# A new order table for every step of a one-core attention and gated-MLP kernel, with its range flag made and loaded ahead of the end

## The chip, the cores and the metric

The kernel runs on one core of one Trainium2 chip. The metric is device microseconds (us) of one execution, as the median of several; the kernel before took 780.11 us in the median of three runs (779.42 to 783.94). Engines are called as in the profile: PE (TensorE, matrix products), PEld (its weight loads), DVE (VectorE), ACT (ScalarE), POOL (GpSimd), SP (SyncE, which issues most DMAs).

## The reference

Eight sequences of 448 tokens, 12 heads of 64. Attention with RMS-normed queries and keys, then a gated MLP with a convolution of three taps along the sequence.

```python
q_n, k_n = rmsnorm(q, g_q), rmsnorm(k, g_k)            # over head_dim = 64
scores = 1 / sqrt(64) * q_n @ k_n.T
attn = exp(scores - max); attn /= attn.sum + 1e-9
x = (attn @ v) heads side by side                       # 8 x 448 x 768
h = relu(x @ w_in)                                      # 768 -> 1024
conv = conv_w[0]*h[t-1] + conv_w[1]*h[t] + conv_w[2]*h[t+1]
out = (h * sigmoid(conv)) @ w_out                       # 1024 -> 768
```

## The kernel before, in words

The unit of attention is a pair of heads of one sequence; there are 48 pairs, six to a sequence, numbered n = 0 to 47. For each pair the kernel loads q, k and v, squares and sums them (`square`, `square_sum`), makes 1/rms in nine small steps (`rsqrt`), scales (`apply_rms`), turns q and k so that the head dimension lies across partitions (`qk_transpose` on PE with `qk_hi`, `qk_lo`; from pair 10 on q by a DMA, `q_hi`, `q_lo`, `q_turn`), forms the scores (`scores`, L862), takes the exponent with a fixed shift (`soft_exp`, L887, on ACT), turns the probabilities, and multiplies by v (`pv`, L1031). Pairs 0 to 9 keep float32 and turn the probabilities on PE (`p_transpose` L939, `p_evac`). Pairs 10 to 47 split every number into two float16 parts (`p_hi`, `p_lo`) and turn them with one DMA per 128 queries (`p_turn`, L931, issued by SP). The row sums are inverted, stored to DRAM and loaded back spread over the partitions (`sum_store`, `sum_load`, `sum_spread`), and `x_scale` applies them.

The MLP of sequence b takes the six finished pairs: `in_part` (L1120) forms x @ w_in for one of eight blocks of 128 features in three float16 products, `in_relu`, `in_conv`, `in_tanh` and `in_gate` make the gated value, `in_hi`, `in_lo` split it, `out_part` (L1189) forms the output for 128 tokens and 384 columns, `out_evac` scales it and `out_store` (L1203) sends it out. Since 448 is three and a half blocks of 128 tokens, the last 64 tokens of an even sequence wait in `carry` and share a block with the first 64 of the next.

PE uses its array in three ways. Products with 128 rows and 128 columns of weights fill it (`in_part`, most of `out_part`, the transposes). `scores` contracts over 64, so two products run at once, one in each half of the rows (64\*128 in the profile, and 64\*64 where a group is half as wide). `pv`, and the block that two sequences share, have 64 columns of weights, so two products run at once, one in each half of the columns (128\*64).

Nothing is scheduled at run time. `plan_qk`, `plan_v`, `plan_attention`, `plan_moe` and `plan_weight` list all 4614 steps, and the string `ORDER` then says, with four characters a step, which step comes next, on which engine it runs and which of the eight PSUM banks it takes. Each engine runs its own steps in that order, and an engine (SP and the ACT queue too, as issuers of DMAs) that must wait holds all that stands behind it. The weights come in at the start as 512 KB pieces (`load`, L438), in 64-bit words whose parts `convert` puts together on DVE.

The attention uses a fixed shift in the exponent; the largest and smallest row sums say afterwards whether that was in range. `sum_check`, `range_turn` (one PE transpose of `top`, L378) and `range_top` (one DVE reduction, L381) make one number of it; `values_load` (L1395) reads it into a register of every engine, and a branch (L1396) skips a general version of the whole kernel, whose code lies between that branch and the end.

```python
    flag = nc.values_load(top[0:1, 2:3].bitcast(I32), min_val=0, max_val=0x7FFFFFFF)
    with tc.If(flag > 0x3F800000):
        general = True
```

Of the kernel before, what the change touches and what calls it, by code (L numbers as in the profile page):

```python
# [9 lines left out]
I32 = mybir.dt.int32  # L10
# [10 lines left out]
    "$2&!$3&!$v&!$w&!$4$!$?$!$x$!%&$!!6&!!!#!$5#!$6#!%^&!$7#!!7&!!0&!!8&!$@#!$P&!$8%!$9%!$y#!$:#!%(#!"  # L21
    "%_&!$A%!$B#!$;#!$z#!%)#!%8&!%r&!$C#!%*#!$<#!$D#!$=#!$E#!%+#!$>#!$F#!${#!%,#!$G#!$|#!!9&!$H#!$J#!"
    "$K!#$I#!!?#!$M#!&:&!!:#!$N!$!1#!$}%!$L$!$O$!$R!B!@#!$~#!$U$!%-#!!;#!!A#!!<#!!>&!!C&!$Q#!%!#!%9#!"
    "&;&!&D&!%.%!%#%!%$#!!D#!!B$!$S!V%%#!$T!l$V!#%s#!%a$!%/%!%0#!!E#!%1#!!I#!!F#!%5#!!J#!%2%!$X$!!=$!"
    "$[$!$_$!%b#!$Y!$!N#!!K#!$]!%&~&!!H&!!M&!(P&!&k&!!O#!$W$!%6!&$Z$!$^$!%7$!!S#!!T#!!P#!!R&!!U#!!W&!"
    "$c$!$f$!%3!(%4$!$a!)$b$!&<$!&=#!%:!.%;!B%<!l$d!($g!)$i$!$l%!$m#!!L$!%>$!%c%!$n#!%d#!!X#!%e#!%f#!"
    "!Y#!%g#!!Z#!!Q$!%h#!%i%!$e$!$h#!%j#!!^#!%k#!%o%!%l%!&E#!(!#!$j!#(Q#!!_#!(R#!%=!:!a#!$o&!!]&!!c&!"
    "!V$!#(&!%A$!!d#!&A#!#)&!(F&!$k$!$p&!$q&!!h#!!e#!!i#!&l&!(G&!)2&!%?!%%B!#%D$!%E!&%@$!%G$!%C$!%H!)"
# [1400 lines left out]
```

## Time and profile before

| | |
|---|---|
| median of three runs | 780.11 us |
| profiled execution, its own time | 784.36 us |
| its span, first to last instruction | 782.6 us |
| PE busy | 749.9 us, 96% |
| DVE busy | 657.2 us, 84% |
| ACT busy | 625.7 us, 80% |
| POOL busy | 345.2 us, 44% |
| granted TensorE clock, mean | 0.996 of full speed |
| DMA, mean | 167 GB/s |

The profiled execution is 4.25 us longer than the median of the runs, and 1.76 us of it lie outside the span. A busy PE is not a PE at its peak: the ends of products are modelled, and a product that starts late inside a run of them shows only in the distance of the starts. Times in the rows are microseconds from the span's start; "xN" merges N like instructions that follow each other; what stands in brackets is idle time before the row and what ended it.

### The profile page before, as it was taken

The page shows a single profiled execution, that of the slowest core. Times are in us where ns is not written, and L with a number is a line of the kernel's source. Part 1 is how long each engine was busy: PE and PEld are TensorE (multiplying, and loading weights), DVE is VectorE, ACT ScalarE, POOL GpSimd, SP SyncE. Part 2 cuts the span into 40 slices and gives each one's busy share as a digit, 9 for nine tenths or more (in the row PEclk, how much of TensorE's full clock was granted, in tenths as well). Part 3 has the DMA queues.
Part 4 walks back from the last instruction along what each step waited for, and adds up shares of the span by engine and source line. Part 5 has one row for each costly group of instructions (what it writes and reads, how often), then busy time and mean ns, then how long its engine had stood idle before and what let it go on. Part 6 is the DMA issues. An engine that isn't in the chain of part 4 may idle for free.

```text
span 782.6 us, 16529 instructions
## 1 busy us (share of the span) xinstructions
PE 749.9 (96%) x5279; PEld 400.0 (51%) x5279; DVE 657.2 (84%) x1592; ACT 625.7 (80%) x1482; POOL 345.2 (44%) x538
## 2 busy tenths in 40 slices
PE   3899999999999989999999999999999999999996
PEld 1455555455545545555545554455445554555553
DVE  6998999999889989898899878997899878974731
ACT  3999899989899868898899778987998778970511
POOL 0154436654366126552465524663465435731200
PEclk9999999999999999999999999999999999999999
DMA  9986664598999999999999999999999988783002
GB/s 239 268 207 185 164 133 96 110 183 185 184 191 185 204 182 180 168 176 206 188 188 187 195 193 184 199 186 180 189 167 180 194 188 155 143 148 83 11 1 85
DMA packets 353428, 130.93 MB, mean 167 GB/s; under 512 B 295708, under 2 KB 349748, under 8 KB 353332
## 3 DMA queue, kind: packets, MB, share of 16 engines
q1 hardware_dynamic: 342928, 120.64, 81.0%
q10 hardware_dynamic: 10404, 9.15, 4.6%
q8 instruction: 43, 0.70, 0.4%
q14 instruction: 53, 0.43, 0.2%
HBM read 48.20 MB, written 11.80 MB: 77 GB/s over the span
## 4 chain that ended last, share of the span: by engine, by line
PE 64%; ACT 13%; DMA 9%; DVE 6%; issue 4%; SPq 1%; POOL 1%; ACTq 0%; DVEq 0%; POOLq 0%
PE bank L1189 23%; PE bank L1120 18%; PE bank L1031 10%; PE bank L862 9%; DMA PT<-PT 3%; DMA PT<-ph 3%; PE bank L939 3%; PE bank L681 2%; ACT PT L267 1%; DMA qkf<-in_q_dram 1%; ACT sq L600 1%; ACT ph L267 1%; DVE ph L279 1%; ACT wi L457 1%; DMA gqk<-in_g_k_dram 1%
## 5 line engine op out<-in xcount | busy, mean ns | idle before, releaser
L1120 PE MATMUL bank<-x,wi 128*128 128x448 f16 x1152 | 229.6, 354 | 2.1 <-DVE kT L731 0.7
L1189 PE MATMUL bank<-wo,gring 128*128 128x384 f16 (+1 forms) x1056 | 196.2, 327 | 0.0
L1120 PEld LDWEIGHTS <-wi 128*128 128x128 f16 x1152 | 111.1, 98 | 109.8 <-issue 14.9
L1189 PEld LDWEIGHTS <-gring 128*128 128x128 f16 (+1 forms) x1056 | 101.4, 99 | 68.3 <-issue 14.2
L862 PE MATMUL bank<-kT,qT 64*128 64x448 f16 (+3 forms) x1072 | 126.4, 388 | 6.1 <-ACT e_(19_2_3546 L887 1.9
L1031 PE MATMUL bank<-PT,vp 128*64 128x448 f16 x836 | 86.7, 354 | 1.0 <-DMA PT<-ph 0.5
L279 POOL TENSOR_TENSOR sq<-qkf,st 112x512 f32<-112x512 f32 (+1 forms) x44 | 46.1, 1060 | 53.5 <-DVE st L637 13.5
L1031 PEld LDWEIGHTS <-vp 128*64 128x64 f16 x836 | 46.2, 110 | 38.9 <-issue 11.7
L862 PEld LDWEIGHTS <-qT 64*128 64x128 f16 (+1 forms) x912 | 33.7, 97 | 56.9 <-issue 34.4
L600 ACT ACTIVATE sq<-qkf 128x1024 f32<-128x1024 f32 (+2 forms) x49 | 49.5, 1022 | 6.6 <-DMA qkf<-in_k_dram 4.5
L681 PE MATMUL bank<-ident,sq 128*128 128x128 f32 (+1 forms) x232 | 35.3, 277 | 13.8 <-DVE st L637 11.1
L609 DVE TENSOR_REDUCE st<-sq 128x16 f32<-128x1024 f32 x38 | 45.3, 1211 | 2.6 <-ACT sq L600 2.6
L1189 PE MATMUL bank<-wo,wi 128*128 128x384 f16 (+1 forms) x192 | 46.9, 326 | 0.0
L279 POOL TENSOR_TENSOR qkf<-sq,qkf 112x512 f16<-112x512 f32 x26 | 30.1, 1162 | 24.6 <-ACT c_(1_0_2529 L271 6.3
L681 PEld LDWEIGHTS bank<-ident,sq 128*128 128x128 f32 (+1 forms) x232 | 26.8, 143 | 24.4 <-issue 16.0
L1189 PE MATMUL bank<-wo,carry 128*64 128x384 f16 x192 | 35.5, 329 | 0.0
L279 DVE TENSOR_TENSOR sq<-qkf,st 112x512 f32<-112x512 f32 (+1 forms) x52 | 34.7, 695 | 0.3
L1031 PE MATMUL bank<-PT,v 112*64 112x448 f32 x160 | 32.3, 545 | 0.0
L774 DVE TENSOR_REDUCE vacc<-v 128x1 f32<-128x512 f32 (+1 forms) x48 | 31.6, 675 | 0.3
L1189 PE MATMUL bank<-wo 128*128 128x384 f16 (+1 forms) x96 | 31.3, 326 | 0.0
L1042 DVE TENSOR_TENSOR x<-bank,rB 128x448 f32<-128x448 f32 x38 | 23.6, 622 | 9.1 <-PE bank L1031 7.7
L279 POOL TENSOR_TENSOR x<-x,x 128x448 f16<-128x448 f32 x22 | 22.8, 1037 | 17.4 <-DVE x L267 4.8
(1911 smaller groups left out, 1714.2 us busy)
## 6 DMA issues: line engine op xcount, KB each, us to landing
qkf<-in_q_dram SPq DMA_DIRECT2D x18, 448.0 KB
wo<-in_moe_w_in_dram SPq DMA_DIRECT2D x12, 512.0 KB
gring<-in_moe_w_out_dram SPq DMA_DIRECT2D x16, 384.0 KB
v<-in_v_dram SPq DMA_DIRECT2D x17, 256.0 KB
qkf<-in_k_dram SPq DMA_DIRECT2D x16, 256.0 KB
qkf<-in_k_dram SPq DMA_DIRECT2D x17, 192.0 KB
PT<-ph SPq DMA_TRANSPOSE x178
qkf<-in_k_dram SPq DMA_DIRECT2D x10, 224.0 KB
```

The costliest lines, as they stand in the source:

```text
L267: (nc.scalar.copy if e == "ACT" else elementwise(e).tensor_copy)(dst, src)
L279: elementwise(e).tensor_tensor(dst, a, b, op=op)
L600: nc.scalar.activation(sq, x, AF.Square)
L609: nc.vector.tensor_reduce(st, sq, axis=AX.X, op=ALU.add)
L681: nc.tensor.transpose(ps[:, t * w : (t + 1) * w], x[:, t], ident[:w, :w])
L774: nc.vector.tensor_reduce(keyed(n, old("vacc", b))[:, i : i + 1], keyed(n, old("v", n)).rearrange("p h t d -> p (h t d)"), axis=AX.X, op=A ...
L862: nc.tensor.matmul(ps[u][o, :S], lhs, rhs, start=(i == 0), stop=(whole(m) or i == 2),)
L939: nc.tensor.transpose(ps[:w, kt * P : (kt + 1) * P], e[:, kt * w : (kt + 1) * w], ident)
L1031: nc.tensor.matmul(ps[HALF[h], :S], lhs, pt[:, k, h * S : (h + 1) * S], start=(i == 0 and j == 0), stop=(i == pvs(n)[-1] and j == NB - 1),)
L1042: nc.vector.tensor_tensor(x, ps, r, op=ALU.mult)
L1120: nc.tensor.matmul(ps[:, :S], wi[:, wl, c, fc * P : (fc + 1) * P], old("x", b * NP + c)[:, xl], start=(i == 0), stop=(i == 3 * NP - 1),)
L1189: nc.tensor.matmul(ps[p0 : p0 + m, :NO2], g, wo[:, wl, fc, half * NO2 : (half + 1) * NO2], start=(i == 0), stop=(i == 3 * NFC - 1),)
```

## The change

`ORDER` is written anew: all 4614 steps and the arithmetic stay, nearly every one stands elsewhere (by 15 places in the mean), 381 steps run on another engine, and banks are given anew. By kind the engines' shares hardly move: `p_hi` has 216 steps on ACT instead of 218 and 37 on POOL instead of 29, `apply_rms` 55 on DVE instead of 52, `out_store` 34 on SP instead of 30, `v_load` 15 on ACT's queue instead of 10. The check of the range stands ahead of the last products of the last sequence, and the register is loaded 30 steps before the end, without the test of its bounds. From the new code on, line numbers are higher by one, and from the moved load on by up to six.

```diff
 ORDER = (
-    "$2&!$3&!$v&!$w&!$4$!$?$!$x$!%&$!!6&!!!#!$5#!$6#!%^&!$7#!!7&!!0&!!8&!$@#!$P&!$8%!$9%!$y#!$:#!%(#!"
...
 WHOLE = 10
 QTURN = 10
+LATE = 30
 SPREAD = 10
...
     with tc.manual_schedule():
-        for step, fn in order:
+        for i, (step, fn) in enumerate(order):
+            if i == len(order) - LATE:
+                flag = nc.values_load(
+                    top[0:1, 2:3].bitcast(I32),
+                    skip_runtime_bounds_check_because="a float that is not negative",
+                )
             taken[:] = placed[step]
...
-    flag = nc.values_load(top[0:1, 2:3].bitcast(I32), min_val=0, max_val=0x7FFFFFFF)
     with tc.If(flag > 0x3F800000):
```

The first place is SP at the start of the program. Before, the first DMAs stand so; `gqk` are the two gain vectors, which every k of the first pair must be multiplied by, and `wo32` is the buffer in which the pieces of w_in arrive.

```order
L562 DMA qkf0_76<-in_k_dram 112x2x256
L578 DMA qkf0_76<-in_q_dram 112x4x128
L562 DMA qkf1_77<-in_k_dram 112x2x256
L576 DMA qkf1_77<-in_q_dram 112x2x128 x2
L438 DMA wo32_84<-in_moe_w_in_dram 128x1024
L562 DMA qkf2_78<-in_k_dram 112x2x256
L438 DMA wo32_84<-in_moe_w_in_dram 128x1024
L1236 DMA gqk_67<-in_g_q_dram 64x1 x2
L1236 DMA gqk_67<-in_g_k_dram 64x1 x2
```

Now the same stretch reads as follows.

```order
L563 DMA qkf0_76<-in_k_dram 112x2x256
L563 DMA qkf1_77<-in_k_dram 112x2x256
L579 DMA qkf0_76<-in_q_dram 112x4x128
L577 DMA qkf1_77<-in_q_dram 112x2x128 x2
L439 DMA wo32_84<-in_moe_w_in_dram 128x1024 x2
L563 DMA v_79<-in_v_dram 112x2x256
L439 DMA wo32_84<-in_moe_w_in_dram 128x1024
L1237 DMA gqk_67<-in_g_q_dram 64x1 x2
L1237 DMA gqk_67<-in_g_k_dram 64x1 x2
```

Three pieces of w_in stand ahead of the gains instead of two, and a load of v in place of a load of k of the same size.

The second place is PE in the first pairs, from the last scores of pair 0 (`kT_177`) through those of pair 1 (`kT_275`); L939 are transposes of probabilities. Before:

```order
L862 MATMUL bank<-kT_177,qT_179 64x448 x2
L862 MATMUL bank<-kT_275,qT_259 64x448 x2
L862 MATMUL bank<-kT_275,qT_259 128x448 x4
L939 MATMUL bank<-ident,e_(0_4_267 112x128 x4
L939 MATMUL bank<-ident,e_(0_5_269 112x128 x4
L939 MATMUL bank<-ident,e_(0_6_301 112x128 x4
L862 MATMUL bank<-kT_275,qT_259 128x448 x2
```

Now, with the same tiles under other numbers:

```order
L863 MATMUL bank<-kT_174,qT_185 64x448 x2
L863 MATMUL bank<-kT_236,qT_228 64x448 x2
L863 MATMUL bank<-kT_236,qT_228 128x448 x2
L940 MATMUL bank<-ident,e_(0_4_264 112x128 x4
L940 MATMUL bank<-ident,e_(0_5_289 112x128 x4
L940 MATMUL bank<-ident,e_(0_6_292 112x128 x4
L863 MATMUL bank<-kT_236,qT_228 128x448 x2
L940 MATMUL bank<-ident,e_(1_0_298 112x128 x4
L940 MATMUL bank<-ident,e_(1_1_314 112x128 x4
L940 MATMUL bank<-ident,e_(1_2_319 112x128 x4
L682 MATMUL bank<-ident,sq_207 128x112 x8
L863 MATMUL bank<-kT_236,qT_228 128x448 x2
```

The scores of pair 1 come in three visits between full-array transposes instead of two. Counted over the whole program, two products that follow each other on PE have different shapes of the array 273 times before and 317 times now.

The third place is the end of SP's program, with the last output stores, the register load and the branch. Before:

```order
L1203 DMA out_0_dram<-c_('o'_7_0_0_9965 128x384
L1203 DMA out_0_dram<-c_('o'_7_3_1_9969 128x384
L1203 DMA out_0_dram<-c_('o'_7_1_1_9972 128x384
L1203 DMA out_0_dram<-c_('o'_7_3_0_9977 128x384
L1395 TENSOR_LOAD top_92
L1395 ISA x2
L1396 COMPARE_AND_BRANCH
```

Now:

```order
L1204 DMA out_0_dram<-c_('o'_7_2_1_9861 128x384
L1385 TENSOR_LOAD top_92
L1204 DMA out_0_dram<-c_('o'_7_3_1_9875 128x384
L1204 DMA out_0_dram<-c_('o'_7_1_0_9898 128x384
L1204 DMA out_0_dram<-c_('o'_7_0_1_9909 128x384
L1204 DMA out_0_dram<-c_('o'_7_1_1_9942 128x384
L1204 DMA out_0_dram<-c_('o'_7_3_0_9940 128x384
L1204 DMA out_0_dram<-c_('o'_7_0_0_9986 128x384
L1401 COMPARE_AND_BRANCH
```

Six of the last stores now stand behind the load; the two instructions of the bounds test are gone, and the branch follows the last store. On PE the load now stands between two products of the last 100, and the transpose of `top` further ahead; nothing follows the last product but the branch.

## Rows read from the trace of the kernel before

**Rows 1.** The page: span, and busy time by engine with its share.
```profile
span 782.6 us, 16529 instructions
PE 749.9 (96%) x5279; PEld 400.0 (51%) x5279; DVE 657.2 (84%) x1592; ACT 625.7 (80%) x1482; POOL 345.2 (44%) x538
```

**Rows 2.** Stretches: us, busy by engine (instructions), granted clock, DMA share, GB/s.
```profile
15.00:40.00 25.00, 21.66 (x121) 12.12 (x123) 24.12 (x57) 23.22 (x63) 4.37 (x9) 1.00 0.93 267
40.00:200.00 160.00, 158.53 (x1054) 87.51 (x1051) 148.56 (x358) 150.27 (x360) 82.89 (x113) 1.00 0.70 157
200.00:400.00 200.00, 195.62 (x1415) 101.50 (x1414) 176.46 (x427) 174.18 (x412) 91.27 (x151) 0.99 1.06 188
400.00:600.00 200.00, 196.27 (x1454) 102.69 (x1454) 179.56 (x423) 175.85 (x417) 105.64 (x172) 1.00 1.05 185
600.00:775.00 175.00, 175.00 (x1235) 94.47 (x1232) 119.60 (x289) 96.64 (x225) 59.64 (x84) 1.00 0.59 118
```

**Rows 3.** PE's waits, 40 to 775 us: us in total, times, longest.
```profile
PE bank L862 <- ACT e_(19_2_3546 L887: 1.9, 1, 1.9
...
PE bank L1031 <- DMA PT<-ph: 0.5, 1, 0.5
PE bank L862 <- DMA qT<-qkf: 0.4, 1, 0.4
```

**Rows 4.** ACT's waits, 40 to 700 us, the two longest.
```profile
ACT ph L267 <- DMA PT<-ph: 10.1, 7, 5.0
ACT e_(19_2_3546 L887 <- DMA rd<-rT: 5.5, 1, 5.5
```

**Rows 5.** PE in order of time, two stretches: start, us, engine, line, tiles, shape, count.
```profile
501.26 2.27 PE L1031 MATMUL bank<-PT,vp 128*64 128x448 f16 x22
503.46 5.85 PE L1120 MATMUL bank<-x,wi 128*128 128x448 f16 x30
509.15 0.60 PE L681 MATMUL bank<-ident,sq 128*128 128x128 f32 x4
...
692.70 1.88 PE L862 MATMUL bank<-kT,qT 64*128 64x448 f16 x18
694.50 2.27 PE L1031 MATMUL bank<-PT,vp 128*64 128x448 f16 x22
696.71 11.88 PE L1189 MATMUL bank<-wo,gring 128*128 128x384 f16 x72
```

**Rows 6.** The start: the chain's wait for the gains, the order of time, DMA rate, a piece's size.
```profile
6.75 6.16 DMA gqk<-in_g_k_dram
...
13.34 0.15 DVE L1239 TENSOR_TENSOR G<-gqk 128x1 f32<-128x1 f32 x1
14.88 4.16 PE L862 MATMUL bank<-kT,qT 64*128 64x448 f32 x12 [0.67 <-ACT qT L267]
...
4.00:13.00 9.00, 0.98 (x4) 0.67 (x4) 6.20 (x29) 2.49 (x5) 0.61 (x3) 1.00 1.00 271
...
wo<-in_moe_w_in_dram SPq DMA_DIRECT2D x12, 512.0 KB
```

**Rows 7.** The end: last product and store; load and branch by line, ns min/median/max, first start.
```profile
775.27 0.33 PE L1189 MATMUL bank<-wo 128*128 128x384 f16 x1
...
776.29 0.33 SPq L1203 DMA_DIRECT2D out_dram<-c_('o'_7_3_0_9977  x1
...
L1395 PEldq TENSOR_LOAD <-top x1: 487/487/487, 776.1 to 776.1; - x1
L1395 SPq TENSOR_LOAD <-top x1: 531/531/531, 776.7 to 776.7; - x1
...
L1396 PEldq COMPARE_BRANCH  x1: 4422/4422/4422, 776.7 to 776.7; - x1
...
L1396 SPq COMPARE_BRANCH  x1: 57/57/57, 777.6 to 777.6; - x1
```

**Rows 8.** SP's own waits: issues of q's turn held by scores of an earlier pair.
```profile
SPq L723 <- PE bank L862: 9.1, 5, 6.5
```

More of the change, by code (lines that the diff above doesn't have):

```diff
@@ new lines @@
+    "$Q#!$}%!$~#!!=$!$X$!%!#!%a$!%##!!E#!%$#!$S!V%5#!%%#!$T!l$[$!$_$!!F#!!I#!%6!#%7$!%9#!%2%!%3!$%4$!"
+    "&<$!%b#!%r&!&D&!!J#!!K#!!L$!!N#!!S#!!O#!!H&!!M&!&=#!%c#!!T#!$V!%!P#!$W$!$Y!&$c$!$Z$!$]!(!U#!$a!)"
+    "%d#!%e%!%s#!&~&!(P&!!R&!!W&!%:!.%;!E$f$!$^$!$i$!$l#!$b$!%f#!!X#!%>$!%g#!!Q$!!Y#!$d!&$g!+$e$!%h#!"
+    "%i%!%A$!$h#!%j#!!V$!%D$!$m#!!Z#!!]&!%k#!!^#!%o%!&k&!&l&!$j!($k$!&E#!(!#!(Q#!#(&!%<!2%l%!&A#!%?!$"
+    "%B!&%@$!%E!%!d#!(R#!%G$!!_#!!a#!!c&!#)&!!e#!!f#!$n#!$o&!!G$!%C$!%F$!&>#!!h#!!i#!%p!+%m!*%J$!%n$!"
@@ new lines @@
+    "!l#!(F&!%q$!(G&!!j#!%=!R!m#!%M$!%H!#%I$!$p&!%K!&%N!%$q&!(S!)(T#!%L$!%O$!!b$!%t!l%u!Q%P$!%S%!&B!&"
+    "%T#!%Q!%!n#!!/%!!p#!!B$!!q#!&C$!!r#!%w$!%R$!!k$!%z$!$r!$!g$!%}$!!#%!%U#!%x!&%{!*)2&!%y$!&?!%%~!)"
+    "({&!!o$!&@$!#*#!#/#!#+#!#0#!#,#!#.&!%V&!#1#!%v!r&F!J%|#!&#$!&!$!![$!!s$!!t#!%Y!#$s#!&m$!&n#!(H%!"
+    "(I#!&$!))3#!$t%!&&$!&(!*&*$!&-$!$u%!&%$!&o%!&p#!&+!$&0#!&q#!&1#!&r#!#4#!&J$!&G!r&s#!&t#!)b&!*>&!"
+    "&.!&&)$!&,$!#5#!&u#!&M$!#6#!#3&!&P$!&v#!&/$!&K!)&L$!&H!E&I!=!u!(&2#!%W&!%X&!(|&!&S$!&w#!&N!&#9#!"
@@ new lines @@
+    "&{#!&x%!!v#!(J%!(M%!&V$!&Q!)&O#!&R$!&T!%%Z#!&U#!#8&!!%%!!x$!)V&!&|!(&y!*&z#!&}$!&W!&)W&!#:#!&Y$!"
+    "(K!)#>#!(N!#&]$!#;#!!y#!#?#!&a#!#@#!(}$!(~#!(#!C($!f&X#!(O$!!z$!(L#!&6!+*+&!%[$!#=&!&Z!#)X$!)Y#!"
+    "(&$!&3&!(*$!&[$!!{%!&b#!)!#!#C#!&^!&((!%#B&!*n&!)##!&c#!#D#!)$#!#E#!#H#!(+!))%#!#I#!#J#!(-$!&_$!"
+    "(%!Q(U!h(0$!()$!)&#!%]#!*,&!(,$!)(%!&4&!)c#!&5&!))#!)*%!*?#!(3$!)+#!#7$!&d&!(.!$(1!%(/#!#F$!(6$!"
+    "(9$!#G&!(<%!#L&!!|$!),%!(2$!*o#!&g!)(4!((5$!!*%!(=#!#M#!)/%!!w#!(7!#(Y$!(:!*&7#!(8$!(;$!(>#!#N#!"
@@ new lines @@
+    "#O#!#R#!(V!8)-!()0!&#S#!#T#!)1#!(Z!+([#!(]$!).$!(W!3(X!:&8$!(a$!(d$!(g$!(^!%(_#!&9%!)Z%!&e&!&f&!"
+    "(j$!)^%!(b!&(m$!*-$!(?&!(c#!(e!#(f$!)4!t)7$!)5!@&h#!(h!&!}#!(p#!#Q&!!~$!&i#!#W#!)_!()a$!&j#!(B!)"
+    ")[!#(i$!#V&!#X#!!)%!*d&!*e&!):$!#!#!##$!(q#!#Y#!!$%!#]#!)]#!(k!+(@&!#^#!(r#!(A&!(n!((l$!(o$!)6!N"
+    ")8!#)=$!)@$!);!++O&!(v!(+P&!)d!@#$#!#_#!*f$!)9$!)C$!#[&!)<#!)>!+)A!#+Q#!)D!&(C#!(D%!(s&!#%$!*g#!"
+    "#<$!)F$!)I$!#c#!#d#!#b&!(t&!(u&!#e#!)?#!#U$!#a$!)e!b)f!F)B#!)E$!)G!##g&!!+%!*.#!(E%!(w#!)h$!)J!&"
@@ L214 @@
+    "UK!!TY#!Tv#!V+!&U0$!V!!%U!#!U##!Ti%!SG$!U1$!U$#!Uw!)U%$!U2#!Tw%!U>$!U&#!U($!U)%!U3#!U4$!Ug!+U?#!"
+    "U@#!UA#!U5#!Uo!*UL$!UM$!UN#!UO#!UB$!UC#!U^!$UP$!UQ#!V3!#UU!(U6#!UD$!UR#!V#!!Uh!!Up!!Ux!!Uy!!V4!!"
+    "V5!!SV$!Uq!!US#!UE%!U_!!Ua!!U7#!Uz!!Ub!!V6!!U{!!U|!!Ui!!Ur!!U}$!V7!!U~$!V$!!V%!!V&!!V(!!V)#!V*&!"
+    "V8!!V9$!V:&!Uc!!Uj!!Uk!!Ul!!Um$!Un&!Ud!!Ue$!Us!!Ut!!Uf&!V,!!V-!!V.!!V/!!V0!!V1$!Uu#!Uv&!UV!!UW!!"
+    "V2&!UX!!UY!!UZ!!U[$!U]&!"
 )
```

360 lines of the change are left out of this document (168 added, 192 removed).

## The prediction

> **What bounds the kernel now.** The page comes first: PE is busy for 749.9 us of 782.6, while ACT and DVE, at 80% and 84%, have room in the mean [rows 1]. So a new order can win only what PE stands still, or what it does slowly while it counts as busy. The view by stretches says where it stands still. From 600 to 775 us PE has no idle time at all. From 40 to 600 us it has 160.00 - 158.53, 200.00 - 195.62 and 200.00 - 196.27, which is 1.5 + 4.4 + 3.7 = 9.6 us. From 15 to 40 us it has 3.3 us, in a stretch where ACT (23.22 of 25) and DVE (24.12 of 25) are full, so that those two set the pace there [rows 2]. Before that lies the start, with the first scores at 14.88 us [rows 6], and behind it the end, from the last product at 775.27 us to the end of the span, about 7 us [rows 1, 7].
>
> PE's own waits say what the 9.6 us are made of. The longest single one, 1.9 us, is a score that waits for ACT to free its bank, and ACT itself had stood 5.5 us behind a DMA of the row sums; 0.5 and 0.4 us more are landings that PE waits for directly [rows 3, 4]. That makes 2.8 us that a longer lead of the DMAs surely could remove. ACT further stood 10.1 us in seven waits for a turned block [rows 4], which is where more of PE's short waits on late exponents can come from.
>
> **What is slow while it counts as busy.** Starts that follow each other show it. Thirty products of 448 columns take 509.15 - 503.46 = 5.69 us, or 0.190 us each, and the transposes behind them, which use the whole array too, begin without a pause. The 22 `pv` products ahead of them run two at a time, so they should take 11 x 0.190 = 2.09 us; they take 503.46 - 501.26 = 2.20. The 18 scores at 692.70 should take 1.71 and take 1.80; the 22 products at 694.50 should take 2.09 and take 2.21 [rows 5]. So each time the array changes between whole, halved by rows and halved by columns, PE loses 0.11, 0.09 and 0.12 us: about 0.105 us, in a stretch where it is never idle.
>
> **The change part by part.**
>
> *The new order of PE.* The products are the same; what changes is how often the shape of the array changes: 273 times before, 317 now, spread over the whole program and not over its start alone. The 44 more cost 44 x 0.105 = +4.6 us. Below, the cost is 0 if all of them fell into waits (PE idles for 9.6 us out of 735 between 40 and 775 us, so few can); above, 44 x 0.12 = +5.3. I take 4.6, since most of the program has PE full [rows 2]. Here two rules of the Trainium skill disagree. "TensorE: Matmul & The Clock Gate", in its Part 2 on what happens when a matmul is issued, says that the draining of one product overlaps the filling of the next, so that only the columns count; by that sentence alone this term would be nothing and the sum 4.6 us lower. "TensorEngine Tiling (Array Packing)", under Key Properties, says that a change of the tiling mode drains the array, and gives no price. The starts in rows 5 bear out the second, with 0.1 us, and I go by them.
>
> *Longer leads for the DMAs.* Measured in PE work between them, at 0.190 us for a product of 448 columns and 0.163 (0.190 x 384 / 448) for one of 384, the last turn of a pair stood less than 4 us ahead of the product that reads it in 7 of 38 pairs, and now does in 2; the median lead of all turns goes from 12.5 to 14.6 us, and that of `q_turn` to its scores from 7.7 to 11.6. The buffer that a turn must have read out before `p_hi` may write it again was due within 3 us 25 times of 260, and now 13 times. So the waits on landings should shrink. Bounds are -9.6 us (all idle time of 40 to 775 us goes) and, since a whole new order can also open new waits, the same upward, +9.6. I take -4.0: the 2.8 us that trace back to DMAs, and a little of the exponents that were late behind the 10.1 us. It is the lower part of what is there, because the leads from scores to exponents became shorter, from 3.8 to 2.8 us in the median. What is late next is then ACT.
>
> *The start.* The gains land at 12.91 us (6.75 + 6.16), G is made from them at 13.34, and the first scores follow 1.54 us later, at 14.88 [rows 6]. SP now issues one more 512 KB piece of w_in ahead of the gains; the load of v is as large as the load of k that it replaces. In that stretch 271 GB/s move, so 0.52 MB more take 1.9 us if transfers are served in the order of issue; the gains then land at 14.8, and scores start at 14.8 + 1.54 = 16.4 instead of 14.88, +1.5 us. Below, it is 0 if the gains pass the weights; above, +1.9. What hides it would have to be slack on ACT or DVE up to 40 us, and these are full [rows 2]. I take +1.5.
>
> *The flag.* At the end SP issues the last store at 776.29, then loads the register (0.53 us), tests it, and branches at 777.6; PE loads for 0.49 us and its branch, with the code behind it, takes 4.42 us from 776.7 [rows 7]. With the load far ahead, SP's branch follows the store at about 776.7, 0.9 us earlier, and PE's follows the last product, 1.4 us earlier; SP is last of the two, so -0.9. The load on PE now stands between two products, where nothing it waits for is late (the reduction stands 159 steps earlier than it did): at worst its 0.49 us are added, at best none, since PE has products queued. I take 0.2. Behind SP's load stand the last six stores, none of which is due then. Together -0.7 (bounds -1.4 and -0.4).
>
> *Engines and banks given anew* (381 steps) change no engine's sum by more than a few dozen operations; they are costed at nothing, since ACT and DVE have idle time in every stretch from 40 us on [rows 2]. Where that cover is gone, between 15 and 40 us, ACT has 43 operations up to the last exponent of pair 1, before and now.
>
> The sum against the profiled span: +4.6 - 4.0 + 1.5 - 0.7 = +1.4, so 784.0 of 782.6, with the time outside it as before. The profiled execution is longer than the median of the runs by 4.25 us; the same difference against that median is 780.11 + 1.4 = 781.5 us.
>
> **The rivals.**
> (a) All idle time from 40 to 775 us goes: +4.6 - 9.6 + 1.5 - 0.7 = -4.2, 775.9 us. For it: every lead of a DMA grew. Against it: several of PE's waits are for ACT and DVE.
> (b) The idle time stays what it was, only elsewhere: +4.6 + 1.5 - 0.7 = +5.4, 785.5 us. For it: the shorter leads of the exponents.
> (c) Slower: SP stands behind PE. SP issues in order, and a turn may be issued only once the product of the pair that had its buffer is done. The first turn of a pair stands with no PE work behind that product in 9 pairs, 4 before, and q's turn directly behind the scores that free its tile in 5 pairs, 1 before. In the trace SP stood 9.1 us in 5 such waits of q's turn, 1.8 each [rows 8]; behind it wait all turns and loads. Nine more are 16.4 us of SP; if half reaches PE, and the gain of 4.0 fails to come, the sum is 5.4 + 8.2 = +13.6, 793.7 us. Against it: turns have 14.6 us of lead in the median. It decides from 2.4 us of added idle time on, which puts the kernel 1% behind.
> (d) The array's change of shape costs nothing, by the overlap of draining and filling: 781.5 - 4.6 = 776.9 us. Against it: rows 5. The Trainium skill's page "TensorE: Matmul & The Clock Gate" is the one that speaks for it.
> (e) As (a), and the ramp up to 40 us loses its 3.3 us of idle time too, with the start unchanged: -4.2 - 3.3 - 1.5 = -9.0, 771.1 us.
>
> **How the numbers follow.** Chances: forecast 0.40, (a) 0.20, (b) 0.20, (c) 0.13, (d) 0.03, (e) 0.04. 1% is 7.8 us, about what a measurement of this kernel can tell from no change: below 772.3 counts as faster, above 787.9 as slower. Faster is (e), with a little of (a): 0.05. Slower is (c) and the upper tail of (b): 0.15. The rest, 0.80, is within 1%. The range runs from just under (a), 775.0, to 789.0, between (b) and (c); outside it lie (e), most of (c) and the lower tail of (a), some 0.2.
>
> **What would show it.** Right: about 0.1 us at each change of shape, as often as counted; the first scores at 16 to 17 us, with G made just behind the gains; PE's waits from 40 to 775 us shorter than 9.6 us in sum, those on DMAs nearly gone; SP's branch within 0.1 us of the last store, and the span's end some 5.4 us behind that store's issue instead of 782.6 - 776.3 = 6.3. Wrong: PE's busy time not above 749.9 us by some 4 to 5 us (then the changes of shape are free), first scores before 15 us, or a stretch between 40 and 775 us with more than 5 us of idle PE.

## The result, and the profile after

The changed kernel takes 787.55 us in the median of eleven runs (785.41 to 793.25) and the kernel before 782.42 us in eleven runs beside them (779.42 to 789.33). The medians differ by 5.1 us. The ratio of the runs on record is 1.0079, with a 95% interval of 1.0054 to 1.0104; it is not the quotient of the medians, which is 1.0066, and stands for 6.2 us (4.2 to 8.1). The forecast was 1.4 us, below that interval; the time lies in the forecast's range, near rival (b), the one in which the idle time of PE stays what it was.

The page of the changed kernel answers to [rows 1].

```profile
span 788.4 us, 16538 instructions
...
PE 754.8 (96%) x5279; PEld 398.3 (51%) x5279; DVE 652.6 (83%) x1595; ACT 625.0 (79%) x1479; POOL 349.0 (44%) x540
```

PE has 4.9 us more busy time with the same 5279 products. The forecast put 4.6 us there, but the two numbers agree by chance, as the stretches show. They answer to [rows 2] (us, busy by engine, granted clock as a share of full speed, DMA share, GB/s); the last four rows are stretches of 4 us.

```profile
15.00:40.00 25.00, 19.91 (x101) 12.49 (x100) 23.50 (x58) 21.20 (x55) 3.78 (x6) 0.88 0.92 259
40.00:200.00 160.00, 159.60 (x1041) 86.60 (x1041) 147.50 (x360) 151.74 (x366) 74.03 (x99) 1.00 0.70 156
200.00:400.00 200.00, 196.64 (x1422) 101.05 (x1420) 177.45 (x430) 171.23 (x408) 103.38 (x169) 0.99 1.04 186
400.00:600.00 200.00, 194.86 (x1418) 99.53 (x1416) 174.40 (x414) 170.21 (x401) 106.72 (x171) 0.99 1.03 185
...
20.00:24.00 4.00, 2.42 (x16) 1.48 (x13) 4.00 (x9) 3.38 (x10) 1.04 (x1) 0.95 0.92 291
24.00:28.00 4.00, 4.00 (x24) 3.04 (x22) 3.53 (x7) 4.00 (x9) 0.00 (x0) 0.62 0.97 274
...
464.00:468.00 4.00, 2.24 (x17) 1.18 (x18) 2.52 (x7) 3.92 (x8) 2.44 (x3) 0.92 1.10 223
468.00:472.00 4.00, 4.00 (x25) 2.35 (x21) 1.56 (x5) 1.91 (x6) 1.70 (x3) 0.65 0.99 215
```

Idle time from 40 to 775 us is 0.40 + 3.36 + 5.14 = 8.9 us (PE is never idle from 600 us on), against 9.6 before; 400 to 600 us has more than the 5 us of idle PE that the prediction had set as a sign of being wrong. Part of the busy time is slow: where the granted clock is 0.65, PE did 0.65 of a full-speed stretch. Busy time times one less the granted clock, summed over stretches of 4 us from 12 us on, gives 6.2 us lost to the lower of the two levels (1.2 GHz), against 1.7 us before, there all of it at 288 to 292 us. So 754.8 - 6.2 = 748.6 us of full-speed work stand against 749.9 - 1.7 = 748.2. Here the lower clock follows a thin stretch (20 to 24 us, where PE is busy for 2.42 of 4.00) or a wait.

PE's waits from 40 to 775 us answer to [rows 3]. They are fewer, nine against seventeen, and longer; of those on DMA landings one is left, of 0.9 us, where there were three of 1.2 us in sum.

```profile
PE bank L1121 <- ACT c_('o'_1_3_0_3582 L272: 2.4, 1, 2.4
PE bank L863 <- ACT e_(31_0_5963 L888: 1.9, 1, 1.9
PE bank L863 <- ACT c_('o'_3_2_0_5977 L272: 1.7, 1, 1.7
PE bank L863 <- DMA qT<-qkf: 0.9, 1, 0.9
```

Behind the three longest stands ACT. Its order of time, in two stretches (ACTq is a DMA that ACT issues; in brackets the idle time before a row and what ended it):

```profile
283.25 0.19 ACT L888 ACTIVATION_READ_ACCUMULATOR e_(19_2_3547<-bank,lift 128x1 f32 x1
286.99 0.64 ACTq L563 DMA_DIRECT2D v<-in_v_dram  x1
287.67 0.56 ACT L268 CAST PT<-e_(19_2_3547 128x448 f16<-128x448 f32 x1 [4.22 <-DMA PT<-ph]
...
289.04 0.57 ACT L272 ACTIVATE c_('o'_1_3_0_3582<-bank,vsc 128x384 f32<-128x384 f32 x1
...
457.07 0.20 ACT L888 ACTIVATION_READ_ACCUMULATOR e_(30_6_5905<-bank,lift 128x1 f32 x1
459.21 0.34 ACTq L1204 DMA_DIRECT2D out_dram<-c_('o'_3_0_1_5773  x1
459.59 0.63 ACT L272 ACTIVATE kT<-bank,G 128x448 f16<-128x448 f32 x1 [2.33 <-DMA qkf<-in_q_dram]
462.56 0.57 ACTq L988 DMA_DIRECT2D row<-rd  x1
463.24 0.63 ACT L888 ACTIVATE e_(31_0_5963<-bank,lift 128x448 f32<-128x448 f32 x1 [3.02 <-DMA qkf<-in_k_dram]
...
465.87 0.58 ACT L272 ACTIVATE c_('o'_3_2_0_5977<-bank,vsc 128x384 f32<-128x384 f32 x1
```

ACT is ready at 283.44 and does nothing until its queue issues a load of v at 286.99, when a turn lands; the eviction of o_1_3_0, four steps behind, frees PE's bank at 289.6. From 457.27 to 463.24 it stands at an output store and at the load of the row sums, 1.9 + 2.3 us. In [rows 4] the 5.5 us of before were of the same kind, at one place: the view puts them down to a load of the row sums, but in order of time ACT issues a load of v and then stands for 3.4 us in front of an output store.

```profile
280.80 0.65 ACTq L562 DMA_DIRECT2D v<-in_v_dram  x1
284.84 0.33 ACTq L1203 DMA_DIRECT2D out_dram<-c_('o'_1_1_1_3341  x1
```

What such an issue waits for is in the trace too. Each DMA reports its landing to a semaphore, a counter that later instructions wait on. The program's 631 DMAs share eight of them, 78 or 79 on each; the first 126 in order of time take them strictly in turn, whichever engine issues. Before they are issued, 572 of the 631 wait for their own semaphore, that is, for the landing of the DMA before on it. The load of v at 286.99 has the semaphore of a turn that SP issued at 282.83 and that landed at 286.97; the output store at 459.21 that of a load of q that SP issued at 452.80, and the load of the row sums at 462.56 that of a load of k that ACT itself had issued at 453.5. The store at 284.84 in the kernel before has that of a turn issued at 279.09. Of six issues at which ACT stands for more than 0.5 us in the changed kernel, five end so. The wait thus comes from the order and the program's eight semaphores, and not from the data that ACT works on.

The start answers to [rows 6] (G in the third row):

```profile
9.91 0.43 DVE L400 TENSOR_SCALAR wi<-wo 128x512 int32<-128x512 int32 x1 [2.12 <-DMA wo<-in_moe_w_in_dram]
13.74 1.73 PE L682 MATMUL bank<-ident,sq 112*128 112x112 f32 x8 [13.74 <-DVE sq L280]
15.26 0.16 DVE L1240 TENSOR_TENSOR G<-gqk 128x1 f32<-128x1 f32 x1 [0.99 <-DMA gqk<-in_g_k_dram]
16.81 1.12 PE L863 MATMUL bank<-kT,qT 64*128 64x448 f32 x2 [1.34 <-ACT qT L268]
```

First scores come at 16.81 instead of 14.88. And the end answers to [rows 7], in order of time and then by line (ns min/median/max, first and last start):

```profile
783.25 0.33 SPq L1204 DMA_DIRECT2D out_dram<-c_('o'_7_0_0_9986  x1
```

```profile
L1385 SPq TENSOR_LOAD <-top x1: 525/525/525, 771.4 to 771.4; - x1
...
L1401 PEldq COMPARE_BRANCH  x1: 3351/3351/3351, 780.6 to 780.6; - x1
...
L1401 SPq COMPARE_BRANCH  x1: 58/58/58, 783.6 to 783.6; - x1
```

From the last store's issue to the end of the span it is 788.37 - 783.25 = 5.1 us, against 782.57 - 776.29 = 6.3.

**Where along the program the time goes.** For one trace, the time minus the PE work started by then says how far PE is behind. A product counts here with the distance at which its kind follows itself in steady runs of the kernel before (0.189 us for `in_part`, 0.163 `out_part`, 0.091 `pv`, 0.087 `scores`, 0.11 a transpose); the sum is the same in every kernel. The table has the difference to the mean of two executions of the kernel before, in us; these two differ by 1.6 us at 60 us and by 0.9 or less in the other columns. "Changes" counts changes of the array's shape. Each row is one execution; that of E2 is the slowest of its twelve, 4.4 us over their median, and the median of the changed kernel is 2.6 us under its row's.

| kernel | changes | 60 us | 285 | 300 | 460 | 480 | last product | span |
|---|---|---|---|---|---|---|---|---|
| changed | 317 | +2.4 | +1.4 | +2.4 | +2.7 | +8.4 | +7.4 | +6.3 |
| E4, flag loaded at the end | 317 | +2.0 | +1.1 | +3.0 | +3.0 | +6.9 | +5.9 | +4.6 |
| E8, two DMA issues later | 317 | +2.9 | +1.4 | -0.7 | +0.6 | +1.0 | +4.0 | +2.7 |
| E7, start as before | 317 | +3.8 | +1.3 | +4.8 | +4.7 | +5.9 | +8.4 | +7.3 |
| E2, before with 44 changes more | 317 | -0.6 | +1.1 | +3.7 | +4.6 | +4.3 | +6.9 | +6.9 |
| E1, changed with 45 fewer | 272 | +4.2 | +8.0 | +7.4 | +14.8 | +17.8 | +19.7 | +18.5 |
| E3, before with 50 fewer | 223 | +1.1 | +2.2 | +0.9 | +17.4 | +17.8 | +27.6 | +27.6 |

The first two rows have the same order of steps from the start to the end. In both, the new order loses 2 us up to 60 us, next to nothing on the 400 us behind, 4 to 6 us in the twenty from 460 to 480, and wins 1 us from there to the last product and 1.2 more at the end.

### The profile page after: what moved, and what is told of

Same layout as the page of the kernel before. It is cut to its first block, busy times and chain, and to the rows that moved or that the text cites. A ratio compares the mean times of both kernels' runs of the same rounds, so it can differ in the third digit from the quotient of the medians.

```text
span 788.4 us, 16538 instructions
## 1 busy us (share of the span) xinstructions
PE 754.8 (96%) x5279; PEld 398.3 (51%) x5279; DVE 652.6 (83%) x1595; ACT 625.0 (79%) x1479; POOL 349.0 (44%) x540
## 4 chain that ended last, share of the span: by engine, by line
PE 77%; DMA 6%; DVE 5%; ACT 5%; issue 3%; POOL 2%; SPq 1%; ACTq 0%; POOLq 0%; DVEq 0%
PE bank L1190 26%; PE bank L1121 22%; PE bank L1032 12%; PE bank L863 11%; PE bank L940 3%; PE bank L682 2%; DMA PT<-ph 2%; DMA PT<-PT 1%; DMA wo<-in_moe_w_in_dram 1%; DMA gqk<-in_g_k_dram 1%; POOL sq L280 1%; DMA qkf<-in_q_dram 1%; DMA row<-rd 1%; ACT ph L268 0%; DMA qT<-qkf 0%
## 5 line engine op out<-in xcount | busy, mean ns | idle before, releaser
L1032 PE MATMUL bank<-PT,vp 128*64 128x448 f16 x836 | 88.6, 360 | 0.0
L280 POOL TENSOR_TENSOR sq<-qkf,st 112x512 f32<-112x512 f32 (+1 forms) x41 | 42.8, 1054 | 63.4 <-issue 18.3
L280 POOL TENSOR_TENSOR qkf<-sq,qkf 112x512 f16<-112x512 f32 x28 | 32.6, 1168 | 15.7 <-DVE ph L280 7.1
L280 DVE TENSOR_TENSOR sq<-qkf,st 112x512 f32<-112x512 f32 (+1 forms) x55 | 37.4, 702 | 0.8 <-POOL sq L280 0.5
L1129 ACT ACTIVATE bank<-bank 128x448 f32<-128x448 f32 x48 | 25.3, 530 | 14.7 <-PE bank L1121 14.5
L268 ACT COPY PT<-bank 112x512 f32<-112x512 f32 x54 | 31.1, 604 | 1.4 <-PE bank L940 1.2
L1017 DVE SCALAR_TENSOR_TENSOR vp<-v,vsc,vp 128x512 f16<-128x512 f32 x38 | 29.4, 777 | 3.0 <-ACT vp L272 2.7
```

Of the source, the lines that this page charges most:

```text
L268: (nc.scalar.copy if e == "ACT" else elementwise(e).tensor_copy)(dst, src)
L280: elementwise(e).tensor_tensor(dst, a, b, op=op)
L1017: nc.vector.scalar_tensor_tensor(vp[:, 1], v32, sc, vp[:, 0], op0=ALU.mult, op1=ALU.subtract)
L1032: nc.tensor.matmul(ps[HALF[h], :S], lhs, pt[:, k, h * S : (h + 1) * S], start=(i == 0 and j == 0), stop=(i == pvs(n)[-1] and j == NB - 1),)
L1129: nc.scalar.activation(ps, ps, AF.Relu, scale=2.0 ** -24)
```

## The experiments

**E1, E2, E3: the price of a change of shape.** Three kernels that differ from one of the two only in the place of some PE steps. In E2, 22 single steps move, as here (PE's order; `kT_938` are scores):

```diff
 L939 MATMUL bank<-ident,e_(6_5_1044 112x128 x4
+L862 MATMUL bank<-kT_938,qT_943 128x448 x2
 L939 MATMUL bank<-ident,e_(6_6_1053 112x128 x4
-L862 MATMUL bank<-kT_938,qT_943 128x448 x6
+L862 MATMUL bank<-kT_938,qT_943 128x448 x4
```

> The kernel before with 22 single PE steps moved past at most 0.8 us of PE work, so that the shape changes 317 times instead of 273. Theory: PE busy 749.9 + 44 x 0.105 = 754.5 us, ratio 1.006. Rival (shape changes free): 749.9 us and ratio 1.000.

Measured: 786.40 us against 783.87, ratio 1.0035 with an interval of 1.0008 to 1.0062, that is +0.6 to +4.9 us. PE is busy for 755.6 us, of which 3.0 are lost to the lower clock; 752.6 at full speed stand against 748.2 and 748.8 in the two executions of the kernel before, 4 us more, or 0.09 us a change. The theory holds and the rival that changes are free falls. The changed kernel shows the price too, where it is read at the changes themselves. From 60 to 775 us, at each change with no wait and no lower clock, the next start comes 0.096 us late in the median, in the kernel before, in E2 and in the changed kernel alike; the sum is 23.6 and 24.0 us in the two executions of the kernel before, 28.0 in E2 and 27.9 in the changed kernel.

E1 goes the other way, from the changed kernel; one of its 27 moves:

```diff
-L863 MATMUL bank<-kT_856,qT_847 128x448 x4
 L940 MATMUL bank<-ident,e_(5_4_868 112x128 x4
 L682 MATMUL bank<-ident,sq_706 128x112 x4
+L863 MATMUL bank<-kT_856,qT_847 128x448 x4
 L1032 MATMUL bank<-PT_70,v 64x448 x8
```

> The changed kernel with 27 short runs of PE steps moved past at most 2.5 us of PE work, so that the shape of the array changes 272 times instead of 317; nothing else is moved. Theory (a change of shape costs 0.105 us each): PE busy 754.8 - 45 x 0.105 = 750.1 us, time 4.7 us below the changed kernel, a ratio to the kernel before of 1.008 - 0.006 = 1.002. Rival (draining overlaps filling, the added busy time of the changed kernel has another cause, such as the lower clock from 22 to 40 us): PE busy stays at 754 to 755, ratio stays at 1.008.

Measured: 803.22 us, ratio 1.0265 (1.0219 to 1.0310), some 15 us slower than the changed kernel. Both theories missed: PE is idle for 21.1 us from 40 to 775 us. E3 moved 35 longer runs in the kernel before, in the same way.

> The kernel before with 35 runs of PE steps moved past at most 2.0 us of PE work each, so that the shape changes 223 times instead of 273. Theory: PE busy 749.9 - 50 x 0.105 = 744.7 us, and time 5.2 us less, ratio 0.993, if PE is what bounds the kernel. Rival 1 (shape changes free): 749.9 us, ratio 1.000. Rival 2 (PE is faster but then waits for what now comes late): PE busy 744.7 and idle from 40 to 775 us above 12 us, ratio 0.997 to 1.000.

Measured: 811.68 us, ratio 1.0362 (1.0312 to 1.0412). Rival 2 had the mechanism and not the size. PE of E3 at one of its places, and the stretches around it:

```profile
339.74 1.31 PE L862 MATMUL bank<-kT,qT 64*128 64x448 f16 x12
343.27 0.35 PE L862 MATMUL bank<-kT,qT 64*128 64x448 f16 x1 [2.23 <-ACT e_(23_2_4322 L887]
344.82 1.27 PE L862 MATMUL bank<-kT,qT 64*128 64x448 f16 x5 [1.20 <-ACT e_(23_3_4335 L887]
```

```profile
200.00:400.00 200.00, 187.25 (x1328) 97.96 (x1324) 169.54 (x416) 167.70 (x396) 88.14 (x145) 0.96 1.01 181
400.00:600.00 200.00, 190.92 (x1345) 99.61 (x1343) 164.69 (x394) 161.40 (x382) 93.35 (x152) 0.97 0.96 175
...
344.00:348.00 4.00, 3.18 (x12) 1.24 (x12) 3.92 (x10) 2.79 (x6) 0.24 (x1) 0.51 0.83 158
```

Scores that stand in one visit fill their banks faster than ACT's exponents empty them: twelve take 1.31 us here, for three and a half banks, and an exponent takes 0.63 us in the rows above, with other steps of ACT between (at this place from 338.8 to 341.9 us). PE is idle for 12.8 + 9.1 us in these two stretches. Waits that end with an exponent make 9.6 us of it, and waits that end with a step of DVE 10.0 us; how much of the latter comes from the moves was not shown. Behind several of these waits the clock falls to 1.2 GHz: 12.2 us of work are lost to it, and PE is busy for 760.1 us with 50 changes fewer. A change of shape has a price, but these two orders with fewer of them are not faster; the products between two visits of scores are time for ACT and DVE.

**E4: the flag.** The register load of the changed kernel goes back behind the last step, with its test of bounds; the range itself is still made early.

```diff
-            if i == len(order) - LATE:
-                flag = nc.values_load(
...
+    flag = nc.values_load(top[0:1, 2:3].bitcast(I32), min_val=0, max_val=0x7FFFFFFF)
     with tc.If(flag > 0x3F800000):
```

> The changed kernel with the register load put back behind the last step, with the test of its bounds, as in the kernel before. Theory (the early load takes SP's load and test off the end): from the issue of the last store to the end of the span 6.3 us instead of 5.1, that is +0.9 to +1.2 us. Rival (the end is set by the landing of the last store and the code behind the branch, whatever comes before): 5.1 us, no change. The idle time of PE from 40 to 780 us, in the same order of the same steps, should be the 8.9 us of the changed kernel again if it comes from the order, and another number if single DMA landings set it.

Measured: 789.00 us, ratio 1.0066 (1.0034 to 1.0097). From the last store to the end it is still 5.0 us. The reason is in the rows of the load, by line:

```profile
L1396 SPq TENSOR_LOAD <-top x1: 481/481/481, 721.4 to 721.4; - x1
...
L1396 SPq SEQ_ASSERT  x1: 33/33/33, 722.2 to 722.2; - x1
```

Although it is written behind the last step, SP's load and its test run at 721 us, ahead of its last eight stores; the loads of ACT and DVE do stand behind their last work, at 781.1 and 775.0 us. So SP's load and test leave the end because the range is made early, and the second half of the edit, the load at the thirtieth step from the end, does nothing that shows. The theory's place was wrong. Idle time from 40 to 775 us is 0.8 + 4.6 + 4.7 = 10.0 us, with waits at the same three places (3.7, 1.7 and 1.7 us): the order sets the places, while the first wait is 1.3 us longer.

**E5, E6, E7: what holds the start.** The load of the gains goes ahead of the third piece of w_in (E5), the first conversion of w_in goes behind the scaling of pair 0 on DVE (E6), and both (E7).

```diff
 v_load 0
+load_g
 load in 2
...
-load_g
...
-convert in 0,0
...
 apply_rms 0,0
+convert in 0,0
```

> The changed kernel with the load of the gains issued directly behind the first load of v, so behind two pieces of w_in instead of three; nothing else moves. Theory of the prediction (the gains set the start): G is made up to 0.99 us sooner, what it waited for the gains in the changed kernel, and the first scores start at 15.8 to 15.9 us instead of 16.81; the first transposes stay at 13.7 to 14.3. Rival (DVE, which stands 2.12 us in front of the first conversion of w_in with the steps of 1/rms behind it, sets the start): first scores stay at 16.6 to 17.0.

> The changed kernel with the first conversion of w_in on DVE moved behind the scaling of q and k of pair 0; the gains stay where they are. Theory (the gains set the start): the first transposes come 2 us sooner, at 11.6 to 12.2, but G still at 15.3 and first scores at 16.6 to 16.9. Rival (DVE sets the start): first scores at 14.7 to 15.0.

> The changed kernel with both moves. Either theory: first scores at 14.7 to 15.2, as in the kernel before (14.88), since both delays are gone; if it stays above 16, a third thing holds the start. The time falls by the same 1.9 us if the ramp to 40 us passes it on, so a ratio of about 1.0055 instead of 1.008; by nothing if ACT and DVE are full up to 40 us anyway. The granted clock from 22 to 40 us, where the changed kernel lost 3.3 us of PE work to half speed, should be full again if a thin stretch of PE before 24 us brings it down.

The rows that answer to the start above, first of E5:

```profile
14.63 1.73 PE L682 MATMUL bank<-ident,sq 112*128 112x112 f32 x8 [14.63 <-DVE sq L280]
15.07 0.16 DVE L1240 TENSOR_TENSOR G<-gqk 128x1 f32<-128x1 f32 x1
16.98 1.12 PE L863 MATMUL bank<-kT,qT 64*128 64x448 f32 x2 [0.62 <-ACT qT L268]
```

E6:

```profile
13.04 1.73 PE L682 MATMUL bank<-ident,sq 112*128 112x112 f32 x8 [13.04 <-DVE sq L280]
16.00 0.16 DVE L1240 TENSOR_TENSOR G<-gqk 128x1 f32<-128x1 f32 x1 [2.09 <-DMA gqk<-in_g_k_dram]
17.55 1.12 PE L863 MATMUL bank<-kT,qT 64*128 64x448 f32 x2 [2.78 <-ACT qT L268]
```

E7:

```profile
13.11 1.73 PE L682 MATMUL bank<-ident,sq 112*128 112x112 f32 x8 [13.11 <-DVE sq L280]
13.89 0.16 DVE L1240 TENSOR_TENSOR G<-gqk 128x1 f32<-128x1 f32 x1
15.46 2.61 PE L863 MATMUL bank<-kT,qT 64*128 64x448 f32 x6 [0.62 <-ACT qT L268]
```

With the gains early G waits for nothing, yet first scores stay at 16.98, since the transposes come late; with the conversion late the transposes come sooner, yet G waits 2.09 us for the gains. Only both together bring first scores to 15.46, a little above what was expected. So the start has two chains of nearly the same length, and each of the theories had one of them. What is won at the first scores is not kept in the profile: E7 is 3.8 us behind at 60 us, against 2.0 to 2.9 in the three rows above it with the new order, and its clock is low again from 32 to 44 us (2.7 us lost). The time doesn't decide it: the ratio, 1.0056 (1.0024 to 1.0088), is the one expected for a start that is passed on, and its interval overlaps that of the changed kernel. E5 and E6 are single runs, read for their rows alone.

**E9: what holds the ramp.** On top of E7, the steps of 1/rms of pairs 2 and 3 stand together on DVE, ahead of the conversions that the new order has between them.

```diff
 rsqrt 2,1
-v_bound 2
-sum_add 0
 rsqrt 2,3
-convert in 6,0
 rsqrt 2,4
...
 rsqrt 2,8
+convert in 5,1
...
+convert in 6,2
```

> The changed kernel with the two moves at the start and with the nine steps of 1/rms of pairs 2 and 3 put together on DVE, ahead of the conversions of w_in, the eviction and the row-sum steps that the new order had put between them. Theory (the ramp is held by pair 2: in the changed kernel its scaling on POOL starts at 34.04 us instead of 32.04, PE stands 1.4 us at its transposes and is so thin until 36 that its clock is halved up to 42): the scaling on POOL starts at 30 to 32 us, transposes of pair 2 at 32 to 34, and at 60 us PE is 2 to 4 us further than in the changed kernel (12.5 us behind its work there, 8.1 in the kernel before); ratio 1.003 to 1.005. Rival (the weights' landings hold the ramp, so what is moved behind is then waited for): still 12 to 14 us behind at 60 us, ratio 1.0055 to 1.008.

Measured: 791.45 us in the median of six runs between 785.84 and 794.93, ratio 1.0111 (1.0063 to 1.0158). The steps of 1/rms were done by 27.9 us, but the scaling on POOL did not follow:

```profile
34.59 2.01 PE L682 MATMUL bank<-ident,sq 112*128 112x112 f32 x8 [3.63 <-POOL sq L280]
33.49 2.04 POOL L280 TENSOR_TENSOR sq<-qkf,st 112x512 f32<-112x512 f32 x2 [6.08 <-DVE wi L400]
```

The kernel ties such a step on POOL to the step of DVE that stands ahead of it in the order (the dependency "shared port" in the code), and ahead of it stood the conversions that had been moved; POOL waited 6.08 us for one of them. At 60 us PE is 2.7 us behind the kernel before, by the measure of the table, where the changed kernel is 2.4: the theory's gain did not come. The profiled execution, 785.84 us, is the fastest of the six, so what made the others slower is not in these rows. The experiment shows that PE stands in the ramp at the transposes of pair 2 (3.63 us here, 1.9 in E7, 1.02 + 0.40 in the changed kernel, none in the first execution of the kernel before and 0.7 in the second). Whether the ramp gets faster when the scaling really comes earlier stays open.

**E8: DMA issues in ACT's queue.**

```diff
 soft_exp 19,2
-v_load 26,1
 p_hi 19,2
...
 soft_exp 19,3
+v_load 26,1
...
-sum_load 29
 soft_exp 31,0
...
 out_evac 3,2,0
+sum_load 29
```

> The changed kernel with two DMA issues of ACT's queue moved behind the evictions and exponents that PE waits for: a load of v (pair 26) and a load of the row sums (pair 29). Theory (PE's idle time in the changed kernel comes from ACT standing in order behind a few DMA issues, 3.5 us at 283 and 2.3 us at 460): PE's waits for the evictions of o_1_3_0 and o_3_2_0 and the exponent e_31_0, 2.4 + 1.7 + 1.9 us, go, idle time of PE from 40 to 775 us falls from 8.9 (10.0 in the run with the flag at the end) to 3 to 5 us, and time by 5 us, ratio 1.002. Rival (whatever stands behind the issue then waits, or the same landings hold other steps): idle stays at 8 to 10 us, ratio 1.007 to 1.008.

Measured: 786.56 us against 784.27, so 2.3 us behind the kernel before instead of 5.1 by the medians. The ratio is 1.0038 (1.0008 to 1.0068), or 3.0 us instead of 6.2; the two intervals overlap, so the size of the gain is uncertain. Waits and stretches of E8:

```profile
PE bank L863 <- DMA qT<-qkf: 1.1, 1, 1.1
PE bank L863 <- ACT c_('o'_3_2_0_5976 L272: 1.0, 1, 1.0
```

```profile
200.00:400.00 200.00, 198.24 (x1458) 102.72 (x1454) 180.18 (x435) 174.49 (x415) 103.14 (x171) 1.00 1.05 190
400.00:600.00 200.00, 195.01 (x1418) 99.54 (x1415) 177.64 (x422) 171.27 (x405) 108.44 (x173) 1.00 1.03 185
```

The waits for o_1_3_0 and e_31_0 are gone, that for o_3_2_0 is 1.0 instead of 1.7, and the clock stays at full speed from 284 to 472 us. In the table E8 is only 1.0 us behind the kernel before at 480 us, of the 8.4 of the changed kernel. It then loses 3.0 us up to the last product, where the changed kernel wins 1.0: later waits take part of it back (1.4 us for a turn behind 480 us, among them). Idle time from 40 to 775 us is 7.1 us, between the 3 to 5 of the theory and the 8 to 10 of the rival. The theory is right about the places and about half of the gain; the rival's reason shows too: the moved load of v now has the semaphore of a later turn, and ACT stands for 1.5 us in front of it until that turn has landed (289.05 us).

**E10: both lessons in the kernel before.** The range is made 127 steps ahead of the end, and the output store at which ACT stood, for 3.4 of its 5.5 us, goes behind three exponents.

```diff
-out_store 1,1,1
 soft_exp 19,2
...
 soft_exp 19,4
+out_store 1,1,1
...
+range_turn
+range_top
 in_part 7,7,0
...
-range_turn
-range_top
```

> The kernel before with two edits: the range is made 127 steps before the end instead of 4, with the register load left where it stands in the code, and one output store of ACT's queue (sequence 1, block 1, half 1) is moved behind the exponents 19_2 to 19_4, which stood 5.5 us behind it. Theory: the end is 5.0 to 5.1 us behind the last store's issue instead of 6.3 (the making of the range, not the place of the load, is what counts); PE's wait for e_19_2 (1.9 us) goes, and with it the half clock at 288 to 292 us (1.7 us); in sum 2 to 4.8 us, ratio 0.994 to 0.998. Rivals: the end stays at 6.3 (then the place of the load counts); the wait returns at another exponent (then only 1.2 us are gained, ratio 0.9985).

Measured: 791.73 us, ratio 1.0107 (1.0065 to 1.0148): slower, mostly by a wait of its own making. DVE in order of time near the end, then PE at 287 us:

```profile
740.47 0.29 DVE L381 TENSOR_REDUCE top<-bank 128x1 f32<-128x128 f32 x1 [10.68 <-PE bank L378]
...
286.89 0.74 PE L862 MATMUL bank<-kT,qT 64*128 64x448 f16 x6 [3.07 <-DMA qT<-qkf]
```

The reduction of the range stands on DVE ahead of work of the last MLP, and DVE is idle for 10.7 us until PE has made the transpose that it needs; the last MLP's gates are late then, and between 700 and 760 us PE falls 6.5 us further behind the kernel before. At 480 us it had been 0.5 us behind, so nearly all of the loss is made at the end. Where the exponent 19_2 no longer holds PE, q's turn does, for 3.07 us at the same time, and ACT stands in front of the moved store again, for 3.7 us. The end is 5.9 us behind the last store, between theory (5.0 to 5.1) and rival (6.3): SP's branch follows the store at once here too, but the stretch behind that branch takes 0.8 to 0.9 us longer than in the changed kernel and E4, for a reason that stays open.

**E11** joins E8 and E9.

> The changed kernel with all moves of the ramp and with the two DMA issues moved behind what PE waits for. Theory (the ramp and the issues in ACT's queue are what the new order lost, and they add): ratio 1.0038 - 0.003 to 0.004 = 1.000 to 1.001, PE 3 us behind the kernel before at most at 480 us. Rival (they don't add, since the DMA queue moves its stalls elsewhere): ratio 1.003 to 1.006.

Measured: 785.87 us, ratio 1.0045 (1.0020 to 1.0071), in the rival's range and no better than E8 alone. E9's moves had brought no gain by themselves, so there was nothing to add, and the rival's reason, stalls that move, is not shown by this. No version here is faster than the kernel before.

**E12: the kernel before once more**, for the scatter of a profile.

> The kernel before, unchanged, profiled once more, to see how far the places of its waits and its granted clock differ from one execution to another: if the order sets them, PE waits again 1.5 to 2.5 us for e_19_2 at 286 us with the clock low behind it, and is 7.5 to 9 us behind its work at 60 us; if single landings set them, they stand elsewhere.

Its span is 781.7 us, its idle time from 40 to 775 us 8.5 us against 9.6, and PE waits for e_19_2 again, 1.3 us instead of 1.9, with the clock low from 284 to 292 us. Waits on single landings differ: 2.4 us on `PT` and 2.0 on `qT` instead of 0.8 and 0.4. So the order sets the place of the longest wait, while waits on landings change: 1.2 us in three before, 4.4 us in five here.

## Why the prediction was right or wrong

**Changes of shape, +4.6: right.** E2 makes 44 of them by themselves, and has 4 us of full-speed PE work more (+0.6 to +4.9 us in the time); read at the changes themselves, the changed kernel has 4 us more too. The Trainium skill's sentence that draining overlaps filling ("TensorE: Matmul & The Clock Gate", Part 2), by which the change would be free, is not borne out by E2, and rival (d) falls with it. But the prediction's sign for it, PE's busy time 4 to 5 us above 749.9, came true in the changed kernel for another reason: 4.5 of the 4.9 us are the lower clock, and E4, with the same order and only 1.1 us lost to the clock, has 751.1. At full speed the whole span hides the price (748.6 us against 748.2); from 60 us to the last product alone, with the start and the ramp left out, busy time at full speed is 2.9 us more than in the mean of the two executions of the kernel before (2.8 in E4).

**Longer leads for the DMAs, -4.0: this step failed.** Idle time went from 9.6 and 8.5 us to 8.9 and 10.0. The table divides it. From 60 to 460 us the new order has 25 changes of shape more (2.6 us) and falls back by only 0.3 to 1.0 us; from 480 us on it has 20 more (2.1 us) and wins 1.0. So waits did shrink there, by 5 us as a difference, a little more than forecast: the idle time that can be read there fell by 2.5 us, and the rest would be starts less late inside the busy time. From 460 to 480 us it loses 3.9 to 5.7 us again, at an output store and a load of the row sums in ACT's queue, in the changed kernel with the lower clock behind them; E8 takes that loss away. The step measured leads from the DMA to PE, and from `p_hi` to its turn. It did not ask what ACT's queue issues between two exponents, although [rows 4] showed 5.5 us of just that: an issue of a DMA holds ACT until the DMA before it on its semaphore has landed, and PE waits for ACT. Of the 2.8 us that the step gave to landings, 1.9 were this: the row names a DMA of the row sums, and ACT stood at an output store. The prediction's own remark that ACT is late next was right, and was not priced.

**The start, +1.5: the size came out partly by luck, the reason was half right.** First scores came 1.9 us later, and PE is 2.0 to 2.4 us behind at 60 us. The gains are one of two chains; E5 to E7 show the other, a conversion on DVE ahead of the 1/rms steps. And the first score alone does not set the ramp: E7 starts nearly as early as the kernel before and is at least as far behind at 60 us as the others. What holds the ramp stays open.

**The flag, -0.7: measured -1.2, by another part of the edit.** Making the range early is enough for it in E4; in E10 the same left the end at 5.9 us. SP's branch did follow the store at once, within 0.1 us, and PE's branch was issued ahead of its last products.

**The rivals.** (b) is what happened in number, with its 785.5 against a measured 780.11 + 5.1 = 785.2 by the medians (786.3 by the ratio). Its reason, the shorter leads of the exponents, is not what the three longest waits show: they stand behind DMA issues of ACT. (c), SP behind PE, did not come: SP stood 5.3 us in six such waits instead of 9.1 in five [rows 8]. The last two columns of the table, in the mean of the changed kernel and E4, divide their +5.4 us of span into +2.2 for the ramp, +4.4 for the 46 changes more behind 60 us at 0.096 us each, about nothing for the waits and the clock behind them (+0.6 and -0.5), and -1.2 for the end; the waits are what the other terms leave, so the sum is no proof of its own.

## What to carry to other kernels

An engine that both computes and issues DMAs stands still at an issue as it does at a wait, so a lead is to be looked at for every issue in its queue, together with what is queued behind it. Where DMAs share a few semaphores in turn, as here, the landing that an issue waits for is that of the DMA that had its semaphore before, possibly of another engine, and moving one DMA in the order changes which one that is. A price per event that is right, such as 0.1 us for a change of shape, does not say that fewer events are faster: what stands between two of them may be the time that another engine needs. And a busy time that comes out as forecast proves nothing until the granted clock of the same stretches has been read.

## What the runs showed of the hardware that was not expected

A wait of PE can cost more than its own time. In the changed kernel 1.9 + 1.7 us of waits from 462 to 466.5 us are followed by a granted clock of 0.92 and 0.65, where 1.6 us of work are lost; in E3, waits of 2.23 and 1.20 us by 0.51, which is the level of 1.2 GHz. It does not do so each time: E4 waits at the same two places, 1.7 us each, and keeps the full clock, as in this row of it.

```profile
468.00:472.00 4.00, 4.00 (x34) 2.40 (x30) 3.25 (x6) 3.60 (x9) 2.15 (x4) 1.00 1.02 217
```

What decides between the two was not settled by these runs. A change of the array's shape costs the same whichever shapes follow each other: read at the changes from 60 us on, each of the twelve successions of the four shapes has a median of 0.09 to 0.10 us, in the kernel before, in E2 and in the changed kernel.
